# One fused attention and mixing kernel: the same instructions in another written order, with fixed PSUM places and buffers

## The chip, the cores and the metric

The kernel runs on one core of a Trainium2 chip. The metric is the device time of one execution in microseconds (us); lower is better. The core has five engines that each work through their own queue in order: TensorE (PE in the profile; its weight loads stand as PEld), VectorE (DVE), ScalarE (ACT), GpSimd (POOL) and SyncE (SP, which here issues the transfers). They wait for each other through semaphores.

## What is computed

Batch 4, 8 heads, sequence 768, head size 64. First a sparse attention, then a Fourier mixing and an MLP over 512 columns:

```
# attention, per batch b and head h; blocks of 64 keys, top_k = 3
k_rep = k.reshape(B, H, 12, 64, D).mean(axis=3)
gate  = einsum('bhsd,bhnd->bhsn', q, k_rep), blocks of the future at -1e9
mask  = (block of key in the 3 best of the query, or its own block) and key <= query
attn  = softmax(where(mask, q @ k.T / sqrt(D), -1e9));  x = attn @ v
# mixing, on x as (B, S, 512)
u   = x + real(fft(fft(x, axis=1), axis=2))
un  = (u - mean(u)) / sqrt(var(u) + 1e-6)
out = u + max(un @ w_ch1, 0) @ w_ch2          # 512 -> 2048 -> 512
```

## The kernel before

The work is cut into 16 pairs of heads (pair P belongs to batch P // 4) and 4 batches. One long string, `ORDER`, names every step; the program reads it once from left to right and emits the instructions of each step, so that the string sets the order in each of the five queues. A step is written `name:indices`. An engine takes its own steps in that order and nothing overtakes. The names are:

- Loads on SP: `Lk`, `Lq`, `Lv` bring k, q and v of a pair (`load`); `LF`, `LT`, `Lc`, `Li` bring constants. `W:c` and `X:c` bring pieces of the two MLP weights through GpSimd's queue (`load_w1`, `load_w2`); `W:0`, `W:1`, `W:2` hold the column tiles 0 to 3, 4 to 9 and 10 to 15 of the first weight.
- Preparing a pair: `tk`, `tq` transpose k and q on PE (pairs 0 to 6; from pair 7 on `kb` and `qc` turn blocks on VectorE instead). `ks` sums k over blocks, `kh` copies the sums (VectorE); `kc` copies k for the scores (ScalarE), `qc` copies q (VectorE) and `qs` copies it on (GpSimd).
- The gate: `g` on PE, then on VectorE `gt`, `gx` (the largest values), `gl:P,0` and `gl:P,1` (which blocks are out) and `gm`, which gives the mask tile mt. From pair 7 on, `K` on GpSimd spreads mt beside q.
- Scores and output: `s:P,i` makes one of six score tiles of a pair in PSUM; `e:P,i` takes the exponential on ScalarE (five wide ones of 1024 columns and a narrow one of 256, `e:P,5`); `d:P,i` clears the part above the diagonal (GpSimd); `vc` casts v (GpSimd); `v:P` multiplies with v on PE; `x:P` divides (VectorE) and writes x.
- Mixing of a batch: `fs`, `fd`, `f` fold x on VectorE; `y:b,h` and `m:b,k` are the two transforms on PE; `ty` (ScalarE) and `tr` (VectorE) copy what `y` made, `u:b,k` adds and sums (VectorE), `xu:b,k` scales (ScalarE). The result is transposed by `xt` on PE and `un` on VectorE for batch 0, by transfers (`un`) for the others. `bn`, `nv`, `nr` make the variance's root, `pg` is a small wait on GpSimd.
- MLP: `w:b,i` makes one of 16 hidden tiles (lines 641 and 643), `r:b,i` its relu (ScalarE, every fourth on VectorE); `c:b,t,h` is the second product, `o` adds and `od` stores.

PSUM holds four places of [128, 1024] fp32. Before, every PSUM tile takes the next of the four in the order of the string (`pst`: one tag, `bufs=4`), so a tile waits until the readers of the fourth tile back are done. SBUF buffers go round likewise: 3 for loads of k and of q, 2 for loads of v, 2 for q in fp32, 4 for mt, 2 for the exponentials (pt, one per pair), 5 for u.

```
    def pst(shape, name, dtype=FP):
        return psump.tile(shape, dtype, tag="ps", name=name)
...
    with tc.manual_schedule(engines={ET.SP, ET.PE, ET.DVE, ET.Activation, ET.Pool}):
        consts_first()
        for x in ORDER.split():
            n, a = x.split(":")
            WORK[n](*[int(i) for i in a.split(",")])
```

## Time and profile before

| | |
|---|---|
| median of 3 runs | 293.21 us (292.3 to 293.62) |
| span of the profiled execution | 290.3 us; the page gives no other time of it |
| granted TensorE clock | 1.00 throughout |
| busy: PE, DVE, ACT, POOL | 274.3, 203.0, 164.4, 113.2 us |
| instructions on PE, DVE, ACT, POOL | 2525, 606, 205, 286 |
| first matmul of the MLP | 65.35 us |

The page's slices divide the span into 40 parts of 7.26 us; a digit is the busy share in tenths. Matmuls are pipelined: a matmul of 512 columns stands with 379 ns, while eight of them in a row take 1.73 us, so PE's work is taken here from the starts of what follows, not from the durations. Rows of the timeline begin with start and duration in us, then engine, line, operation, output and inputs, and the count merged into the row; what stands in brackets is the idle time just ahead and what ended it. A row of a window gives the window, its length and the busy time and instructions of PE, PEld, DVE, ACT and POOL, then the granted clock, the share of the DMA engines and GB/s.

### The profile page before, as it was taken

How to read it: one execution, taken by the hardware profiler on the slowest of the kernel's cores; microseconds unless marked ns; L12 is line 12 of the kernel's file. 1: busy time of each engine (PE TensorE's matmuls, PEld its weight loads, DVE VectorE, ACT ScalarE, POOL GpSimd, SP SyncE). 2: the span in 40 equal slices, each digit the busy share in tenths (PEclk: the TensorE clock that was granted, in tenths of full speed). 3: DMA queues.
4: the chain of work that ended last, by engine and by line, in shares of the span. 5: the costliest groups of instructions: out<-in, count | busy, mean ns of one | idle time of the engine just before them, and what ended most of it. 6: DMA issues, size and time to landing. Idle time of an engine off the chain costs nothing.

```text
span 290.3 us, 6581 instructions
## 1 busy us (share of the span) xinstructions
PE 274.3 (94%) x2525; PEld 167.7 (58%) x2525; DVE 203.0 (70%) x606; ACT 164.4 (57%) x205; POOL 113.2 (39%) x286
## 2 busy tenths in 40 slices
PE   7696976899999999999999999999999999999995
PEld 3554664575656665565576457646766654656443
DVE  2899988999789988689988668609691559202122
ACT  3676878877579666579888505687143231263000
POOL 2246470614988815845760489414400001100000
PEclk9999999999999999999999999999999999999999
DMA  9999999899999399964900004541000024000034
GB/s 200 267 236 263 172 215 178 140 180 162 154 189 205 76 183 212 130 131 117 213 17 2 0 0 148 109 92 73 2 2 0 36 76 108 0 2 0 0 147 181
DMA packets 121423, 33.52 MB, mean 115 GB/s; under 512 B 114160, under 2 KB 118192, under 8 KB 121392
## 3 DMA queue, kind: packets, MB, share of 16 engines
q1 hardware_dynamic: 115728, 28.47, 46.0%
q0 software_dynamic: 3664, 4.19, 9.2%
q10 hardware_dynamic: 2000, 0.44, 0.7%
q8 instruction: 20, 0.33, 0.5%
q14 instruction: 11, 0.09, 0.1%
HBM read 28.63 MB, written 6.29 MB: 120 GB/s over the span
## 4 chain that ended last, share of the span: by engine, by line
PE 79%; DVE 13%; ACT 5%; issue 2%; DMA 1%; DVEq 0%; ACTq 0%
PE c L668 27%; PE h L641 19%; PE h L643 10%; PE sc L426 7%; PE av L461 4%; ACT pt L443 4%; DVE u L578 2%; PE yp L531 2%; DVE kr L306 2%; DVE q L328 2%; PE warmps L705 1%; PE sc L421 1%; DVE mx L378 1%; PE c L660 1%; PE g L354 1%
## 5 line engine op out<-in xcount | busy, mean ns | idle before, releaser
L443 ACT ACTIVATE pt<-sc 128x1024 f16<-128x1024 f32 (+1 forms) x96 | 83.5, 918 | 26.1 <-PE sc L426 14.6
L641 PE MATMUL h<-unT,w 128*128 128x512 f16 x256 | 84.5, 379 | 0.0
L668 PE MATMUL c<-w_sb,hT 128*128 128x512 f16 x368 | 83.0, 379 | 0.2 <-ACT pt L443 0.2
L643 PE MATMUL h<-unT,w 128*128 128x256 f16 x256 | 69.7, 272 | 0.0
L449 POOL TENSOR_SCALAR_AFFINE_SELECT pt<-pt 128x256 f16<-128x256 f16 x96 | 38.5, 424 | 68.0 <-ACT pt L443 45.9
L668 PEld LDWEIGHTS <-hT 128*128 128x128 f16 x368 | 35.7, 98 | 40.6 <-issue 0.7
L653 ACT ACTIVATE hT<-h 128x768 f16<-128x768 f32 x48 | 37.4, 809 | 34.7 <-PE h L643 34.6
L641 PEld LDWEIGHTS <-w 128*128 128x128 f16 x256 | 25.0, 98 | 29.5 <-issue 0.7
L680 DVE SCALAR_TENSOR_TENSOR u<-c,rs,u 128x512 f32<-128x512 f32 (+1 forms) x25 | 17.3, 724 | 29.9 <-PE c L668 25.6
L651 DVE TENSOR_SCALAR hT<-h 128x768 f16<-128x768 f32 x16 | 15.2, 948 | 19.4 <-PE h L643 19.4
L643 PEld LDWEIGHTS <-w 128*128 128x128 f16 x256 | 25.0, 98 | 3.9
L426 PE MATMUL sc<-qk 96*128 96x512 f16 (+3 forms) x144 | 26.0, 306 | 0.1
L224 POOL TENSOR_SCALAR_AFFINE_SELECT qk<-q 64x768 f16<-64x768 f32 (+1 forms) x25 | 21.0, 843 | 12.8 <-DVE q L328 12.1
L590 ACT ACTIVATE x<-u,nm 128x512 f16<-128x512 f32 x24 | 16.0, 714 | 16.3 <-DVE nm L584 16.2
L224 POOL TENSOR_SCALAR_AFFINE_SELECT qk<-mt 32x160 f16<-32x160 f16 x72 | 23.0, 340 | 2.6 <-DVE mt L398 0.9
L461 PEld LDWEIGHTS <-pt 128*128 128x128 f16 x672 | 22.2, 97 | 2.8 <-issue 1.1
L461 PE MATMUL av<-v,pt 128*128 128x65 f16 x672 | 23.0, 193 | 0.5 <-ACT pt L443 0.3
L421 PE MATMUL sc<-qk 64*128 64x512 f16 (+3 forms) x112 | 14.9, 306 | 5.4 <-ACT pt L443 3.2
L578 DVE SCALAR_TENSOR_TENSOR u<-mx,x 128x512 f32<-128x512 f32 x24 | 15.6, 685 | 5.2 <-PE mx L565 5.2
L224 POOL TENSOR_SCALAR_AFFINE_SELECT v<-nat 128x768 f16<-128x768 f32 x16 | 14.7, 920 | 8.6 <-DMA nat<-in_v_dram 8.6
L426 PEld LDWEIGHTS <-qk 96*128 96x128 f16 x144 | 12.7, 97 | 8.6 <-issue 0.9
L544 ACT CAST ty<-yp 128x772 f16<-128x772 f32 x8 | 8.0, 1036 | 16.7 <-PE yp L531 16.4
(98 smaller groups left out, 349.2 us busy)
## 6 DMA issues: line engine op xcount, KB each, us to landing
nat<-in_v_dram SPq DMA_DIRECT2D x16, 384.0 KB, 5.0
...
```

The costliest lines, as they stand in the source:

```text
L224: nc.gpsimd.affine_select(out=out, in_=in_, pattern=[[0, i] for i in n], base=0, channel_multiplier=0, compare_op=ALU.is_ge, fill=0.0)
L421: nc.tensor.matmul(ps[:, e, co:co + q1 - q0], qk[hs[e], 1, XW(P), 128 * jt:128 * jt + 128], qk[hs[e], 0, XW(P), q0:q1], start=(co == 0), s ...
L426: nc.tensor.matmul(ps[:, e, co:co + q1 - q0], qk[0:96, e, 1, 128 * jt:128 * jt + 128], qk[0:96, e, 0, q0:q1], start=True, stop=True)
L443: nc.scalar.activation(out=d["pt"][:, o:o + 2 * n].rearrange("p (e c) -> p e c", e=2), in_=d["sc", i][:, :, 0:n], func=AF.Exp, scale=0.125)
L449: nc.gpsimd.affine_select(out=dg, in_=dg, pattern=[[0, 2], [1, 128]], base=0, channel_multiplier=-1, compare_op=ALU.is_ge, fill=0.0)
L461: nc.tensor.matmul(av[:, e, 66 * st:66 * st + 65], pt[:, co:co + 128], vv[:, e, jt, 0:65], start=(cnt == 0), stop=(cnt == 20))
L578: nc.vector.scalar_tensor_tensor(out=u_b[:, k2, :].rearrange("p (m two) -> p two m", two=2), in0=mps[:, k2, :].rearrange("p (two m) -> p t ...
L641: nc.tensor.matmul(hp[:, 0:512], w1s, unT[:, dt, 0:512], start=(dt == 0), stop=(dt == NDT - 1))
L643: nc.tensor.matmul(hp[:, 512:768], w1s, unT[:, dt, 512:768], start=(dt == 0), stop=(dt == NDT - 1))
L653: nc.scalar.activation(out=hT, in_=hp, func=AF.Relu)
L668: nc.tensor.matmul(c_ps[b, g[0]][:, st - g[0], :], h_t[b, it][:, 128 * st:128 * (st + 1)], w2_sb[:, it, :], start=(it == 0), stop=(it == N ...
L680: nc.vector.scalar_tensor_tensor(out=o, in0=ps, scalar=st_t[b][1][:, st:st + 1], in1=o, op0=ALU.mult, op1=ALU.add)
```

## The change

The string holds the same 1002 steps before and after, each once. They stand in another order from the first load on, in all five queues. A step may now carry `@n`, and the new variable `place` holds that number while the step is emitted. It names the PSUM place (four tags with one buffer each, in place of one tag with four), the load buffer (0 to 2 for k and for q, 0 and 1 for v), the buffer of q in fp32 (0, 1), of mt (0 to 3), of the exponentials (0, 1) and of u (0 to 4). The numbers of buffers and their sizes are as before. The string is cut here after the part around the first tiles of the MLP.

```diff
@@ -110,70 +110,78 @@


 ORDER = """
-Lk:1 Lq:1 Lk:2 Lq:2 Lq:3 Lk:3 tk:0 ks:0 kh:0 iz:1 iz:0 tq:0 kc:0 qc:0 g:0 tq:1 gt:0 gx:0 gl:0,0
-gl:0,1 gm:0 qc:1 tk:1 kc:1 tk:2 kc:2 ks:1 qs:0 qs:1 Lq:4 Lv:0 Lk:4 Lv:1 kh:1 s:0,1 ks:2 s:0,3 tq:2
-qc:2 g:1 kh:2 e:0,1 s:0,0 s:0,5 gt:1 s:0,4 s:0,2 tk:3 e:0,3 e:0,5 g:2 gx:1 gl:1,0 Lq:5 Lk:5 gl:1,1
-gm:1 s:1,4 tq:3 s:1,3 e:0,0 tq:4 gt:2 tk:4 e:0,4 ks:3 qc:3 gx:2 gl:2,0 s:1,0 kh:3 qc:4 gl:2,1 s:1,1
-e:0,2 g:3 ks:4 e:1,4 gm:2 Lv:2 d:0,3 qs:2 d:0,4 d:0,2 vc:0 vc:1 d:0,0 d:0,1 d:0,5 Lv:3 Lq:6 LF:0
-Lq:7 Lk:6 Lk:7 LT:0 v:0 s:1,5 s:2,4 e:1,3 kc:3 tq:5 e:1,0 s:2,5 s:2,2 e:1,1 gt:3 kc:4 gx:3 gl:3,0
-kh:4 x:0 e:1,5 g:4 s:1,2 s:2,3 e:2,4 e:2,5 qc:5 gl:3,1 e:2,2 gt:4 e:1,2 tk:5 gx:4 gm:3 ks:5 e:2,3
-s:2,1 e:2,1 qs:4 qs:3 vc:2 d:1,4 d:2,5 qs:5 d:1,0 d:1,3 d:1,5 d:1,2 d:1,1 fs:0,0 kh:5 gl:4,0 fs:0,1
-gl:4,1 v:1 x:1 s:3,1 s:2,0 s:3,4 g:5 kc:5 s:3,3 e:3,1 e:3,4 s:3,0 qc:7 gm:4 e:2,0 tq:6 e:3,0 s:3,5
-e:3,5 e:3,3 gt:5 s:3,2 s:4,1 e:3,2 fs:1,1 gx:5 fs:1,0 gl:5,0 Lv:4 Lq:8 Lk:8 Lv:5 Lc:0 d:3,1 d:2,1
-d:2,2 d:3,4 d:2,0 d:3,5 d:3,0 d:2,3 d:2,4 vc:3 d:3,2 d:3,3 gl:5,1 kb:7 v:2 e:4,1 kc:7 gm:5 ks:7 v:3
-s:4,5 e:4,5 s:4,0 qc:6 x:2 s:5,4 e:5,4 s:5,5 s:4,4 x:3 s:5,2 s:4,3 s:5,0 tk:6 e:5,5 fs:2,0 kh:7
-fs:3,1 fs:3,0 fs:2,1 fd:3,0 fd:2,0 fd:2,1 fd:3,1 f:0,2 f:0,0 f:0,1 y:0,0 e:4,4 ks:6 f:0,3 y:0,1
-e:5,2 s:5,3 e:5,0 e:4,0 tr:0,0 e:4,3 tr:0,1 m:0,2 kc:6 ty:0,0 g:7 ty:0,1 kh:6 m:0,1 u:0,2 g:6 u:0,1
-s:4,2 gt:6 e:5,3 m:0,0 s:5,1 xu:0,2 e:4,2 xu:0,1 xt:0,1 gx:6 e:5,1 u:0,0 xu:0,0 Lk:9 Lq:9 W:0 W:1
-d:4,0 pg:0 vc:4 d:4,4 d:5,0 qs:6 d:4,3 d:4,1 W:2 d:4,2 d:4,5 gl:6,0 gl:6,1 v:4 un:0,1 gm:6 s:6,3
-gt:7 xt:0,0 xt:0,2 s:6,1 s:6,4 x:4 e:6,3 s:6,2 e:6,2 un:0,0 un:0,2 gx:7 gl:7,0 gl:7,1 kb:8 w:0,6
-r:0,6 w:0,12 e:6,1 w:0,11 w:0,2 qc:8 ks:8 gm:7 kb:9 kh:8 g:8 r:0,12 s:6,0 r:0,11 s:6,5 w:0,0 e:6,4
...
+Lk:1@1 Lk:2@2 tq:0@1 Lq:1@1 tk:0@2 iz:1 qc:0@0 tk:1@3 ks:0 Lq:2@2 qs:0 kh:0 ks:1 g:0@0 Lk:4@0
+tk:2@1 gt:0 kc:1 ks:2 kc:0 tq:1@0 Lq:4@0 gx:0 kc:2 gl:0,0 iz:0 qc:1@1 tq:2@3 Lk:3@1 gl:0,1 kh:1
+qs:1 gm:0@0 s:0,0@2 qc:2@0 s:0,4@1 Lk:7@2 e:0,0@0 g:1@0 qs:2 s:0,3@3 e:0,4 gt:1 s:0,1@2 d:0,0
+tk:4@0 e:0,3 kh:2 gx:1 d:0,4 g:2@1 gl:1,0 e:0,1 Lv:0@0 tk:3@3 gl:1,1 gt:2 kc:4 Lq:3@1 gm:1@1
+s:1,2@1 gx:2 kc:3 s:0,5@2 ks:4 e:0,5 e:1,2@1 s:0,2@2 d:0,5 ks:3 tq:4@0 Lv:1@1 e:0,2 s:1,4@1 gl:2,0
+Lk:5@0 vc:0 qc:4@1 s:1,3@3 e:1,4 s:1,0@2 d:0,3 kb:7 d:0,2 e:1,0 tq:3@0 d:1,2 gl:2,1 d:0,1 v:0@1
+kh:3 e:1,3 gm:2@2 Lq:5@2 qc:3@0 d:1,3 LF:0 s:1,5@2 s:2,3@3 kh:4 e:1,5 vc:1 x:0 Lv:3@0 g:3@0 e:2,3@0
+s:2,2@2 qs:3 gt:3 s:1,1@1 e:2,2 s:2,5@3 Lq:6@0 g:4@0 fs:0,1 gx:3 e:2,5 tq:5@2 e:1,1 d:2,5 gl:3,0
+d:1,0 s:2,1@3 gt:4 d:1,5 tk:5@1 e:2,1 d:1,1 qc:5@0 s:2,4@0 d:1,4 s:2,0@3 e:2,4 gl:3,1 Lv:2@1 fs:0,0
+v:1@2 gm:3@3 vc:3 ks:5 Lk:6@1 e:2,0 s:3,4@0 qs:5 gx:4 s:3,0@3 e:3,4@1 gl:4,0 d:2,1 x:1 d:2,2 e:3,0
+Lq:7@1 s:3,3@0 d:2,0 kh:5 ks:7 vc:2 g:5@2 kc:5 s:3,1@3 gl:4,1 e:3,3 d:2,3 gt:5 tq:6@1 d:2,4 LT:0
+d:3,4 s:3,5@2 gm:4@0 e:3,1 v:2@0 Lk:10@0 qs:4 qc:6@0 e:3,5 d:3,0 gx:5 s:3,2@3 d:3,3 s:4,2@2 d:3,1
+x:2 e:3,2 s:4,0@1 e:4,2@0 gl:5,0 s:4,1@3 d:3,2 qc:7@1 d:3,5 v:3@0 e:4,0 W:0 fs:2,0 Lv:5@0 gl:5,1
+fs:2,1 e:4,1 gm:5@1 s:4,4@2 fs:1,0 tk:6@1 Lv:4@1 x:3 e:4,4 s:5,0@3 fd:2,0 kc:6 s:5,2@0 fs:1,1
+s:4,3@2 fs:3,1 e:5,0@1 fs:3,0 fd:2,1 fd:3,0 s:4,5@3 e:4,5 fd:3,1 e:4,3 s:5,4@3 f:0,1 e:5,4 f:0,0
+s:5,5@2 e:5,5 y:0,0@3 f:0,2 Lk:9@1 ks:6 f:0,3 s:5,3@2 ty:0,0 y:0,1@1 kb:10 vc:4 e:5,2 Lq:9@2 tr:0,0
+d:4,2 kc:7 s:5,1@0 d:4,4 tr:0,1 d:5,2 m:0,2@3 W:1 kh:6 kh:7 ks:10 ty:0,1 Lk:8@2 d:4,3 d:4,1 u:0,2@0
+e:5,1 d:5,4 m:0,1@1 d:4,0 e:5,3 m:0,0@0 u:0,1@1 xu:0,2 g:6@3 d:5,3 d:5,0 xt:0,2@2 d:4,5 u:0,0@2
+xu:0,1 d:5,5 d:5,1 v:4@1 W:2 gt:6 xu:0,0 xt:0,1@0 qs:6 un:0,2 xt:0,0@3 un:0,1 qs:7 g:7@2 un:0,0
+Lc:0 x:4 w:0,6@0 vc:5 gx:6 Lq:8@0 w:0,5@3 r:0,6 kb:8 w:0,0@1 gl:6,0 r:0,5 gt:7 ks:8 w:0,2@0 gl:6,1
+kb:9 w:0,8@2 r:0,2 gm:6@2 gx:7 r:0,0 s:6,5@3 s:6,1@0 kh:10 kh:8 r:0,8 gl:7,0 v:5@1 e:6,1@0 gl:7,1
+qc:9@0 s:6,3@2 Lv:6@1 e:6,5 gm:7@3 K:7 s:6,2@0 e:6,3 x:5 w:0,11@3 Lv:7@0 e:6,2 bn:0,0 s:6,4@2
+s:6,0@1 qc:8@1 e:6,4 w:0,7@0 Lq:10@1 r:0,11 qs:8 kc:9 g:8@2 bn:0,1 w:0,12@3 e:6,0 gt:8 d:6,5 d:6,1
+Li:0 s:7,2@2 r:0,7 X:0 r:0,12 w:0,15@1 ks:9 e:7,2@1 d:6,0 qs:9 s:7,0@0 Lk:11@1 kh:9 r:0,15 s:7,5@3
+w:0,14@2 e:7,0 pg:0 gx:8 vc:7 e:7,5 s:7,3@1 r:0,14 gl:8,0 d:6,2 g:9@0 gl:8,1 s:7,4@3 d:6,3 fs:4,0
+X:1 w:0,3@2 qc:10@1 e:7,4 d:6,4 gt:9 e:7,3 d:7,2 s:7,1@3 d:7,5 gm:8@0 w:0,10@0 bn:0,3 e:7,1 d:7,3
+d:7,0 bn:0,2 d:7,4 kc:10 w:0,4@1 vc:6 gx:9 d:7,1 bn:0,4 v:6@3 r:0,10 K:8 Lk:12@0 r:0,3 r:0,4 v:7@0
+kc:8 gl:9,0 fs:5,0 x:6 w:0,9@1 gl:9,1 w:0,1@2 gm:9@1 K:9 r:0,9 x:7 s:8,5@3 g:10@1 fs:6,1 r:0,1
+w:0,13@0 bn:0,5 e:8,5@0 gt:10 s:8,2@2 r:0,13 kb:11 s:9,4@3 s:8,0@1 e:8,2 fs:7,0 c:0,0,0@0 fs:4,1
+gx:10 e:8,0 gl:10,0 nv:0 e:9,4@1 s:9,1@2 fs:7,1 Lv:9@0 nr:0 s:8,1@1 fs:6,0 fs:5,1 s:9,2@3 fd:6,1
+e:8,1 c:0,0,1 Lq:11@2 gl:10,1 fd:7,0 e:9,1 fd:6,0 fd:7,1 e:9,2 s:9,3@1 f:1,1 s:8,3@2 f:1,0 c:0,1,0
+e:8,3 Lv:8@1 f:1,3 e:9,3 Lq:13@0 f:1,2 s:9,0@3 d:9,4 s:9,5@2 ks:11 d:9,3 s:8,4@1 qs:10 c:0,1,1
+e:8,4 gm:10@2 kh:11 kb:12 e:9,5 e:9,0 d:8,3 y:1,1@1 Lk:13@2 d:8,0 o:0,1 kc:11 pg:1 c:0,2,0@2 d:9,0
+tr:1,1 vc:9 qc:11@0 Lq:12@1 ty:1,1 d:8,4 d:9,5 y:1,0@3 d:8,1 o:0,0 d:8,5 g:11@1 od:0,1 qs:11 ty:1,0
...
 assert PT_W == 5376 and len(COL) == 42

@@ -206,13 +214,15 @@
     dr = {n: nc.inline_tensor(C[n], name=f"c_{n}") for n in C}

     cpool = ctx.enter_context(tc.tile_pool(name="cst", bufs=1))
-    psump = ctx.enter_context(tc.tile_pool(name="psum", bufs=4, space=bass.MemoryType.PSUM))
+    psump = ctx.enter_context(tc.tile_pool(name="psum", bufs=1, space=bass.MemoryType.PSUM))
     apool = ctx.enter_context(tc.tile_pool(name="attn", bufs=2))
     bpool = ctx.enter_context(tc.tile_pool(name="bat", bufs=1))
     spool = ctx.enter_context(tc.tile_pool(name="small", bufs=3))

+    place = [0]
+
     def pst(shape, name, dtype=FP):
-        return psump.tile(shape, dtype, tag="ps", name=name)
+        return psump.tile(shape, dtype, tag=f"ps{place[0]}", name=name)

     def ctile(shape, dtype, name):
         return cpool.tile(shape, dtype, tag=f"c_{name}", name=name)
@@ -265,11 +275,11 @@
         b, hp = divmod(P, NP)
         src = (q, k, v)[who]
         if who == 2:
-            t = apool.tile([128, 2 * NST, 64], FP, tag="nat2", name=f"nat2_{P}", bufs=2)
+            t = apool.tile([128, 2 * NST, 64], FP, tag=f"nat2{place[0]}", name=f"nat2_{P}", bufs=1)
             eng.dma_start(t, src[b, 2 * hp:2 * hp + 2].rearrange("e (st p) d -> p (e st) d", p=128))
             nat[P, 2] = t
             return
-        t = apool.tile([128, NST, 2, 64], FP, tag=f"nat{who}", name=f"nat{who}_{P}", bufs=3)
+        t = apool.tile([128, NST, 2, 64], FP, tag=f"nat{who}{place[0]}", name=f"nat{who}_{P}", bufs=1)
         nat[P, who] = t
         if P in BLK[who]:
             nat[P, who] = t = t.rearrange("p st e d -> p (st e d)")
@@ -320,7 +330,7 @@
                 nc.scalar.copy(out=qk[0:64, e, 1, :], in_=ps[64 * e:64 * e + 64])

     def a_q32(P):
-        q32 = apool.tile([128, S], FP, tag="q32", name=f"q32_{P}")
+        q32 = apool.tile([128, S], FP, tag=f"q32{place[0]}", name=f"q32_{P}", bufs=1)
         pairs[P]["q32"] = q32
         if P in BLK[0]:
             nc.vector.transpose(out=q32, in_=nat[P, 0])
@@ -394,7 +404,7 @@

     def g_back(P):
         d = pairs[P]
-        d["mt"] = apool.tile([128, 288 if P < NX else 160], F16, tag="mt", name=f"mt_{P}", bufs=4)
+        d["mt"] = apool.tile([128, 288 if P < NX else 160], F16, tag=f"mt{place[0]}", name=f"mt_{P}", bufs=1)
         nc.vector.transpose(out=d["mt"], in_=d["lt"])

     def stage_K(P):
@@ -438,7 +448,7 @@
     def s_exp(P, i):
         d = pairs[P]
         if "pt" not in d:
-            d["pt"] = apool.tile([128, PT_W], F16, tag="pt", name=f"pt_{P}")
+            d["pt"] = apool.tile([128, PT_W], F16, tag=f"pt{place[0]}", name=f"pt_{P}", bufs=1)
         o, n = SC_OFF[i], sum(q1 - q0 for (_, q0, q1) in SC_TILES[i])
         nc.scalar.activation(out=d["pt"][:, o:o + 2 * n].rearrange("p (e c) -> p e c", e=2),
                              in_=d["sc", i][:, :, 0:n], func=AF.Exp, scale=0.125)
@@ -567,7 +577,7 @@

     def m_u(b, kp):
         mps, x_b = m_ps[b, kp], x_t[b]
-        u_t[b, kp] = u_b = bpool.tile([128, 2, DM], FP, tag="u_b", name=f"u{kp}_{b}", bufs=5)
+        u_t[b, kp] = u_b = bpool.tile([128, 2, DM], FP, tag=f"u_b{place[0]}", name=f"u{kp}_{b}", bufs=1)
         if b not in st_t:
             un_t[b] = bpool.tile([128, NDT, S], F16, tag="unT", name=f"unT_{b}", bufs=1)
             st_t[b] = [bpool.tile([128, *sh], FP, tag=n, name=f"{n}_{b}", bufs=2)
@@ -688,7 +698,7 @@
     def consts_first():
         for who in (1, 0):
             src = (q, k)[who]
-            t = apool.tile([128, NST, 2, 64], FP, tag=f"nat{who}", name=f"nat{who}_0", bufs=3)
+            t = apool.tile([128, NST, 2, 64], FP, tag=f"nat{who}{place[0]}", name=f"nat{who}_0", bufs=1)
             nat[0, who] = t
             for e, eng in ((0, nc.sync), (1, nc.scalar)):
                 eng.dma_start(t[:, :, e, :], src[0, e].rearrange("(st p) d -> p st d", p=128))
@@ -765,6 +775,8 @@
     with tc.manual_schedule(engines={ET.SP, ET.PE, ET.DVE, ET.Activation, ET.Pool}):
         consts_first()
         for x in ORDER.split():
+            x, _, at = x.partition("@")
+            place[0] = int(at or 0)
             n, a = x.split(":")
             WORK[n](*[int(i) for i in a.split(",")])

```

## The prediction

> **What bounds the kernel now.** I read the page's busy lines and slices first, then TensorE's work in two windows, then the chain and the timelines of the stage before the second window.

> ```profile
> PE 274.3 (94%) x2525; PEld 167.7 (58%) x2525; DVE 203.0 (70%) x606; ACT 164.4 (57%) x205; POOL 113.2 (39%) x286
> PE   7696976899999999999999999999999999999995
> DVE  2899988999789988689988668609691559202122
> ...
> 0.00:65.35 65.35, 52.83 (x769) 36.00 (x770) 56.01 (x192) 47.12 (x58) 26.21 (x64) 1.00 1.03 205
> 65.35:287.00 221.65, 221.34 (x1758) 131.66 (x1756) 146.52 (x415) 117.25 (x147) 87.02 (x222) 1.00 0.43 89
> ...
> 62.35 0.39 PE L421 MATMUL sc<-qk 64*128 64x384 f16 x4
> 62.88 1.07 PE L597 MATMUL xt<-id,x 128*128 128x128 f16 x16
> 64.02 0.39 PE L421 MATMUL sc<-qk 64*128 64x256 f16 x4
> 65.35 0.39 PE L641 MATMUL h<-unT,w 128*128 128x512 f16 x1
> ```

> From 65.35 us on, when the first matmul of the MLP (`w:0,6`) starts, PE is busy for 221.3 of 221.7 us at full clock. A changed order can save nothing there; it can only add waits. Before that PE is busy for 52.8 of 65.35 us while VectorE is at eight or nine tenths in most slices. So the change is worth what it does to one moment: how early `w:0,6` can start, less the PE work that it leaves until afterwards.

> That work is counted in the two orders. Ahead of `w:0,6` both have the 14 transposed loads, `g:0` to `g:7`, all score tiles of pairs 0 to 5, `v:0` to `v:4` and the whole Fourier part of batch 0. The old order also has four score tiles of pair 6 (`s:6,3`, `s:6,1`, `s:6,4`, `s:6,2`), the new one none. By the last four rows these take 62.88 - 62.35 = 0.53 and 65.35 - 64.02 = 1.33, together 1.86 us, which move behind the start.

> **When `w:0,6` starts in the new order.** No instruction is added or removed, so all durations come from this trace. I carry the new order along the engines' queues, each item starting when its queue is free, its inputs are there and its PSUM place has been read out.

> ```profile
> 5.06 1.79 PE L297 MATMUL tp<-id,nat 128*128 128x128 f32 x12
> 8.77 0.69 PE L347 MATMUL g<-q,kr 128*32 128x288 f32 x8 [1.92 <-DVE q L328]
> 12.50 2.08 ACT L443 ACTIVATE pt<-sc 128x1024 f16<-128x1024 f32 x2
> ...
> 6.57 0.89 DVE L306 TENSOR_REDUCE kr<-tp 128x12 f32<-128x768 f32 x1
> 7.67 0.95 DVE L328 COPY q<-tp 128x768 f32<-128x768 f32 x1
> 9.52 0.48 DVE L361 STREAM_TRANSPOSE gt<-g 128x288 f32<-128x288 f32 x1 [0.90 <-PE g L347]
> 10.24 0.72 DVE L378 MAX8 mx<-gt 128x8 f32<-128x8 f32 x9
> 11.56 0.48 DVE L398 STREAM_TRANSPOSE mt<-lt 128x288 f16<-128x288 f16 x1
> ```

> *To the first exponential: later.* `tq:0` now goes ahead of `tk:0`, and its load lands near 6.0 (in the old order `tq:0` follows `tk:0` in the 12 transposes from 5.06). VectorE then does `qc:0`, `ks:0`, `ks:1` (0.9 each) from 7.05 to 9.8, with `g:0` on PE from 9.05; `gt:0` 0.75, `ks:2` 0.9, `gx:0` 0.7, `gl:0,0` 0.3, `qc:1` 0.9, `gl:0,1` and `kh:1` 0.3, `gm:0` 0.45: mt is there at 14.2, and `e:0,0` starts at 14.7 against 12.50. `ks:1`, `ks:2` and `qc:1` are done by then, which the old order still had ahead of it.

> ```profile
> 12.50:40.30 27.80, 23.43 (x364) 15.49 (x363) 26.74 (x96) 22.52 (x27) 15.00 (x30) 1.00 1.05 229
> ...
> 38.46 2.21 ACT L443 ACTIVATE pt<-sc 128x256 f16<-128x256 f32 x3 [0.36 <-PE sc L433]
> 42.29 1.02 ACT L443 ACTIVATE pt<-sc 128x1024 f16<-128x1024 f32 x1 [1.61 <-PE av L461]
> ...
> 46.26 5.88 ACT L443 ACTIVATE pt<-sc 128x1024 f16<-128x1024 f32 x7 [1.11 <-PE sc L433]
> ...
> 40.73 2.73 PE L461 MATMUL av<-v,pt 128*128 128x65 f16 x84 [0.33 <-ACT pt L443]
> ...
> 43.76 0.96 DVE L221 TENSOR_TENSOR x<-av,rcp 128x768 f16<-128x768 f32 x1
> ```

> *Pairs 0 to 3: caught up.* ScalarE is the measure here. From `e:0,0` to `e:3,2` it has 20 wide exponentials, 4 narrow ones and 3 copies of k; at 0.91 (the six wide and one narrow of the 5.88 us row, the narrow one at about 0.3), 0.3 and 0.75 that is 21.6 us. In the old order this stretch ends at 38.46 + 2.21 = 40.67, after 28.2 us; the window shows ScalarE busy for 22.5 of its first 27.8 us. In the new order I find waits of 0.35 before `e:1,4`, 0.3 before `e:1,5`, `e:2,3` and `e:3,4`, 0.45 before `e:2,1`, 0.35 before `e:2,4` and 0.95 before `e:3,2` (its score tile stands behind `v:2`): 3.0 us. So it ends at 14.7 + 21.6 + 3.0 = 39.3. It waits less because pair 4 is transposed ahead of pair 3 and score tiles of the next pair stand between those of the last one.

> Behind it the old order runs `v:2` and `v:3` together (2.73 us from 40.73), so `x:2` and `x:3` queue on VectorE and the last ends at 43.76 + 0.96 = 44.7; `e:4,1` waits 1.61 us for `v:2`, which still reads its buffer. The new order has `v:2` at 36.6 and `x:2` done at 39.3. GpSimd's `d:3,2` and `d:3,5` let `v:3` go at 40.3; it ends at 41.6, `x:3` at 43.15, and `e:4,2` runs straight after `e:3,2`. By the end of this part 1.55 us are won.

> ```profile
> 44.99 0.89 DVE L221 TENSOR_TENSOR sd<-x 128x384 f16<-128x384 f16 x3
> 45.80 1.96 DVE L221 TENSOR_TENSOR zw<-sd 128x768 f16<-128x768 f16 x4
> 47.79 0.56 DVE L221 TENSOR_TENSOR fg<-zw 128x762 f16<-128x762 f16 x1
> 52.08 2.04 DVE L550 CAST tr<-yp 128x768 f16<-128x768 f32 x2
> 55.36 0.68 DVE L578 SCALAR_TENSOR_TENSOR u<-mx,x 128x512 f32<-128x512 f32 x1
> 63.88 1.28 DVE L602 COPY unT<-xt 128x1024 f16<-128x1024 f16 x2
> ...
> 43.21 1.67 ACT L320 CAST qk<-nat 64x768 f16<-64x768 f32 x2
> 53.15 2.05 ACT L544 CAST ty<-yp 128x772 f16<-128x772 f32 x2 [0.31 <-DVE tr L550]
> 56.90 1.33 ACT L590 ACTIVATE x<-u,nm 128x512 f16<-128x512 f32 x2 [0.82 <-DVE nm L584]
> ...
> 51.72 1.35 PE L531 MATMUL yp<-fs_sb,fg 128*128 128x193 f16 x14
> ```

> *From `x:3` to `w:0,6`: shorter.* The old order takes 65.35 - 44.7 = 20.65 us. In the new one VectorE folds from 43.15 (four `fd` at 0.47, three `fs` at 0.27, two `f` at 0.56) to 47.0. ScalarE runs `e:4,2` to `e:4,4` until 43.1, `kc:6` and `e:5,0` until 44.75, waits 0.55, then `e:4,5`, `e:4,3`, `e:5,4` until 47.4, which frees the place of `y:0,0`: 47.6 to 49.1. `s:5,3`, then `y:0,1` until 50.6. ScalarE: `ty:0,0` to 50.2, `e:5,2` to 51.1, `kc:7` 1.6 to 52.7, `ty:0,1` to 53.6. That copy sets the end: `m:0,1` from 53.8 to 54.65, `m:0,0` to 55.55 (0.87 each); `m:0,2` and `u:0,2` were done by 54.4. `u:0,1` to 56.3 and `u:0,0` to 57.7 (1.4 each: two of 0.68 and the mean); `xu:0,0`, behind the other two at 1.25, to 59.15; `xt:0,0` to 59.85; `un:0,0`, the last of three at 0.6, to 60.65. `w:0,6` starts 0.2 later (63.88 + 1.28 to 65.35 in the old one): 60.8, 17.65 us after `x:3`. The old order is held up by `m:0,0`, which stands on PE behind `g:6` and `s:4,2`, and by four score tiles of pair 6 and `x:4` on VectorE ahead of the last two `un`.

> *The sum.* 65.35 - 60.8 = 4.55 us earlier, 1.86 us of scores behind it: 2.7 us won. After it I followed 45 us of handovers, to `y:1,0`. Inputs arrive 0.1 to 4 us ahead, but at eight places PE takes a PSUM place within 0.1 us of its last reader's end (`w:0,15` after `e:6,0`, `s:7,1` after `e:7,4`, `s:9,2` after `e:9,4` and the like). No row shows such tight handovers at that place; nothing is gained by them, and the bound above is below. I charge 0.4 us, nearest to the second window's total of 0.3 us of idle. Net 2.3 us: span 290.3 - 2.3 = 288.0. The median of the runs, 293.21, lies 2.9 us above the span (the page has no other time for the profiled execution); I keep that distance: 290.9 us, 0.8% less.

> Loads change places too: `Lk:7` and `Lk:10` come early, `Lq:3` and `Lv:0` behind `Lk:7`. On SP they keep ahead of their first use by 2 us or more as I count them, and their cover is the exponentials; `Lk:8` waits for `kc:7`, with `Lc` and `Lq:8` queued behind, first needed 9 us later. The one load that could end last is a rival.

> **The rivals.**

> ```profile
> PE sc L421 <- ACT pt L443: 3.2, 5, 1.6
> POOL v L224 <- DMA nat<-in_v_dram: 8.6, 3, 6.3
> ...
> 41.91 1.71 POOL L735 DMA_DIRECT2D w<-in_moe_w_ch_dram  x2
> 55.35 0.76 POOL L735 DMA_DIRECT2D w<-in_moe_w_ch_dram  x1
> DMA to landing us min/median/max: 7.9/8.0/10.9
> ```

> *Tight places.* Each of the eight handovers after `w:0,6` waits for ScalarE. In the first stage such waits are 3.2 us in 5, 0.64 each. At 0.3 each they cost 2.4 us instead of 0.4 and the time is 292.9, no change; at 0.64 they cost 5.1 and it is 295.6. Against it: ScalarE is busy for 117 of the 222 us of the second window, and the old order, also fed by four places, shows no such loss there. Chance 0.22, most of it on no change.

> *The weights last: slower.* `W:1` brings the columns of `w:0,6`. In the old order it is the second issue from 41.91, 22 us ahead of need. In the new one it stands on GpSimd behind `vc:4` and `d:5,2` and goes out at about 51.5; with 7.9 to 10.9 us to landing it is there at 59.4 to 62.4, against a need at 60.8. The worst of this costs 62.4 + 0.2 - 60.8 = 1.8 us. But if `vc:4` waits for its load of v as long as the longest wait of its kind (6.3 us), `W:1` goes out at 57.8, lands at 65.7 to 68.7, and PE stands idle: 290.9 + 5.1 to 8.1 = 296.0 to 299.0. It decides from a landing after 60.6, and eats the whole gain from one after 62.9. Against it: `Lv:4` is issued near 36, seven us before I have `vc:4` reach it. Chance 0.12.

> [...] The rows above show 7.9 us at the least, so I keep its chance.

> **How the numbers follow.** Forecast 0.66; tight places 0.22; weights 0.12. Low end: no charge for handovers and half of ScalarE's 3.0 us of waits gone as well, 2.7 + 1.5 = 4.2: 289.0. High end: it takes in no change and the start of both rivals' slower parts, 293.9. About 0.5% is what a measurement can tell here, 291.7 to 294.7. Faster holds the forecast less its upper edge, 0.64; within, 0.23 (tight places at 0.3, part of a late `W:1`); slower, 0.13.

> **What would show it.** The first exponential near 14.7; `v:2` near 36.6, ahead of the last exponential of pair 3; `x:3` ending near 43; the first h near 60.8 with no score of pair 6 ahead of it; PE at 9.9 or more of 10 us from 61 on; `W:1` landed before the last `un`. I am wrong if h starts after 63, if PE is idle for over 2 us behind it, or if VectorE, not ScalarE, holds back `y:0,0`.

## The result, and the profile after

The change makes the kernel slower: 296.6 us (median of four executions, 295.38 to 297.88) against 292.79 us for the kernel before beside it, a ratio of 1.0124 with a 95% interval of 1.0087 to 1.0161. 290.9 us had been forecast, with a range from 289.0 to 293.9. Ratios here and below leave out, on both sides, executions that took over 1.5% more than the fastest of the same kernel. The profiled execution took 295.38 us, with a span of 293.7 us; in that of before the span was 290.3 us.

These lines of the page of the changed kernel answer to those of before; the windows are in the second fence (the last two count PE alone), PE's timeline in the third.

```profile
PE 275.3 (94%) x2525; PEld 168.5 (57%) x2525; DVE 197.0 (67%) x606; ACT 164.4 (56%) x205; POOL 113.5 (39%) x286
PE   6699897869999999997999999999999999999995
DVE  2989998997998886998678756923562560750131
...
PEclk9999997999999999999999999999999999999999
```

```profile
64.06:290.30 226.24, 223.98 (x1792) 132.55 (x1791) 141.86 (x434) 118.71 (x148) 83.08 (x214) 1.00 0.43 89
...
44.91:48.33 3.42, 1.44 (x22) 1.00 1.26 243
48.33:51.74 3.41, 3.41 (x30) 0.50 1.03 183
```

Three things are new. The clock row has a 7: from 48.33 to 51.74 us TensorE was granted half its clock, where the trace of before shows 1.00 throughout. PE's row has a 6 at 59 to 66 us, where the row of before has 9, and a 7 at 132 to 140 us. And from the first h tile to its last step PE is idle for 226.24 - 223.98 = 2.26 us instead of 0.31.

```profile
45.41 0.23 PE L431 MATMUL sc<-qk 64*128 64x128 f16 x2 [0.70 <-ACT pt L453]
...
46.19 0.39 PE L431 MATMUL sc<-qk 64*128 64x512 f16 x2 [0.50 <-ACT pt L453]
...
47.10 0.23 PE L431 MATMUL sc<-qk 64*128 64x128 f16 x2 [0.33 <-ACT pt L453]
...
48.02 1.05 PE L541 MATMUL yp<-fs_sb,fg 128*128 128x193 f16 x7 [0.64 <-ACT pt L453]
...
50.31 0.53 PE L541 MATMUL yp<-fs_sb,fg 128*128 128x193 f16 x2
50.78 0.61 PE L431 MATMUL sc<-qk 64*128 64x384 f16 x4
...
62.14 0.40 PE L607 MATMUL xt<-id,x 128*128 128x128 f16 x4 [1.54 <-ACT x L600]
...
64.06 0.38 PE L651 MATMUL h<-unT,w 128*128 128x512 f16 x1 [0.51 <-DVE unT L612]
...
71.49 0.22 PE L443 MATMUL sc<-mt,indz 64*128 64x32 f16 x4 [0.61 <-DVE mt L408]
```

`y:0,0` starts at 48.02 and the tile behind it at 50.78: 2.76 us for what takes 1.62 at full clock (in e1 below). `w:0,6` starts at 64.06, 1.29 us earlier than before and not 4.55.

```profile
58.15 0.17 DVE L594 TENSOR_SCALAR nm<-sm 128x2 f32<-128x2 f32 x1
...
59.56 1.76 DVE L594 TENSOR_SCALAR nm<-sm 128x2 f32<-128x2 f32 x1
61.24 0.47 DVE L371 STREAM_TRANSPOSE gt<-g 128x288 f32<-128x288 f32 x1
...
67.48 0.98 DVE L311 STREAM_TRANSPOSE nat<-nat 128x768 f32<-128x768 f32 x1 [1.71 <-DMA nat<-in_k_dram]
```

```profile
58.91 0.76 POOL L745 DMA_DIRECT2D w<-in_moe_w_ch_dram  x1
59.68 2.50 POOL L234 TENSOR_SCALAR_AFFINE_SELECT qk<-q 128x768 f16<-128x768 f32 x3
```

```profile
119.74 2.56 SPq L287 DMA_DIRECT2D nat<-in_q_dram  x4
122.41 2.60 SPq L615 DMA_TRANSPOSE unT<-x  x2
125.11 0.54 SPq L279 DMA_DIRECT2D nat<-in_v_dram  x1
125.75 5.29 SPq L615 DMA_TRANSPOSE unT<-x  x4
```

```profile
PE h L653 <- DMA unT<-x: 1.6, 1, 1.6
```

These are the timelines of VectorE, GpSimd and SP's queue, and a line of the waits (in total, times, longest). On VectorE the two elements of nm, 0.17 us after `u:0,1`, take 1.76 us after `u:0,0`, while GpSimd issues `W:2` and runs `qs:6` and `qs:7`. Both `xu:0,0` and the 1.54 us of idle PE at 62.14 wait for them. Later VectorE waits 1.71 us for the load `Lk:8` with the mask of pair 6 queued behind it, and SP's queue sends `Lq:15` ahead of the transposes `un:1`, for which PE then waits 1.59 us.

The account: the last step, `c:3,5,0`, starts at 288.34 us instead of 285.21, 3.12 us later. That is 1.29 us won ahead of h, 1.86 us of score tiles moved behind it, and a remainder of 2.55 us of new waits behind it (the 1.59, the 0.61, and small ones). The expectations below count otherwise: against an estimate of the work alone, from start to start (220.25 us in the new order, 218.38 in the old), PE is idle for 4.03 us between `w:0,6` and the last step (4.35 to the very end), against 1.48 in before.

### The profile page after: what moved, and what is told of

The parts are those of the page before. It is cut to its first block, busy times and chain, and to the rows that moved or that the text cites. A ratio compares the mean times of both kernels' runs of the same rounds, so it can differ in the third digit from the quotient of the medians.

```text
span 293.7 us, 6588 instructions
## 1 busy us (share of the span) xinstructions
PE 275.3 (94%) x2525; PEld 168.5 (57%) x2525; DVE 197.0 (67%) x606; ACT 164.4 (56%) x205; POOL 113.5 (39%) x286
## 4 chain that ended last, share of the span: by engine, by line
PE 79%; DMA 7%; ACT 6%; DVE 3%; SPq 2%; issue 1%; ACTq 0%; DVEq 0%
PE c L678 27%; PE h L651 17%; PE h L653 9%; PE sc L436 7%; PE av L471 6%; ACT pt L453 5%; DMA nat<-in_k_dram 4%; DMA nat<-in_q_dram 2%; PE yp L541 2%; PE sc L431 2%; SPq L287 2%; PE tp L307 2%; PE sc L443 1%; DMA unT<-x 1%; PE mx L575 1%; PE mx L574 1%
## 5 line engine op out<-in xcount | busy, mean ns | idle before, releaser
L653 PE MATMUL h<-unT,w 128*128 128x256 f16 x256 | 69.8, 273 | 1.6 <-DMA unT<-x 1.6
L663 ACT ACTIVATE hT<-h 128x768 f16<-128x768 f32 x48 | 37.6, 812 | 47.4 <-PE h L653 47.1
L459 POOL TENSOR_SCALAR_AFFINE_SELECT pt<-pt 128x256 f16<-128x256 f16 x96 | 37.1, 410 | 26.1 <-ACT pt L453 22.5
L234 POOL TENSOR_SCALAR_AFFINE_SELECT qk<-q 64x768 f16<-64x768 f32 (+1 forms) x25 | 20.5, 823 | 12.4 <-DVE q L338 10.9
L471 PE MATMUL av<-v,pt 128*128 128x65 f16 x672 | 22.5, 193 | 0.0
L231 POOL TENSOR_TENSOR t<-vr,rs 128x6 f32<-128x6 f32 x12 | 3.2, 270 | 47.5 <-DVE rs L631 46.9
```

Source lines behind the costliest of these rows:

```text
L234: nc.gpsimd.affine_select(out=out, in_=in_, pattern=[[0, i] for i in n], base=0, channel_multiplier=0, compare_op=ALU.is_ge, fill=0.0)
L459: nc.gpsimd.affine_select(out=dg, in_=dg, pattern=[[0, 2], [1, 128]], base=0, channel_multiplier=-1, compare_op=ALU.is_ge, fill=0.0)
L471: nc.tensor.matmul(av[:, e, 66 * st:66 * st + 65], pt[:, co:co + 128], vv[:, e, jt, 0:65], start=(cnt == 0), stop=(cnt == 20))
L653: nc.tensor.matmul(hp[:, 512:768], w1s, unT[:, dt, 512:768], start=(dt == 0), stop=(dt == NDT - 1))
L663: nc.scalar.activation(out=hT, in_=hp, func=AF.Relu)
```

## The experiments

The four causes were first mended one at a time. In the diffs a stretch of the string is broken into lines so that the moved steps stand alone.

**e1: the clock.** A step `sa` makes a score tile once more in its old tile.

```diff
 s:4,3@2
+sa:5,2@0
 fs:3,1 e:5,0@1 fs:3,0 fd:2,1 fd:3,0 s:4,5@3
+sa:5,2@0
 e:4,5 fd:3,1 e:4,3 s:5,4@3
+sa:5,2@0
 f:0,1 e:5,4 f:0,0 s:5,5@2
+sa:5,2@0
 e:5,5 y:0,0@3
```

> The changed kernel, with the score tile s:5,2 computed again, into the same place and with the same values, behind s:4,3, s:4,5, s:5,4 and s:5,5: about 0.57 us of TensorE work in each of the four gaps (0.70, 0.50, 0.33 and 0.64 us) between 44.7 and 48.0 us; nothing waits for the repeats but TensorE itself. Theory (the idle stretch halves the clock): the granted clock stays 1.0 from 43 to 53 us, y:0,0 takes 1.5 us instead of 2.8 and ends at 49.5-49.7, ty:0,0 starts 1.2 earlier, w:0,6 starts at 62.7-63.2 instead of 64.06, and the span falls by 0.9-1.3 us, to 292.4-292.8. Rival (the clock dip comes from something else than idleness, such as the load of the stretch before): the dip to half stays at 48.3-51.7, y:0,0 still takes 2.6-2.8, and the span is the same or up to 0.5 us more.

```profile
44.10:47.51 3.41, 3.03 (x58) 1.00 1.22 221
```

```profile
48.02 0.76 PE L541 MATMUL yp<-fs_sb,fg 128*128 128x193 f16 x7 [0.23 <-ACT pt L453]
...
49.38 0.33 PE L541 MATMUL yp<-fs_sb,fg 128*128 128x193 f16 x2
...
68.67 0.38 PE L651 MATMUL h<-unT,w 128*128 128x512 f16 x1 [1.20 <-DVE gt L376]
```

First a window, then PE's timeline. The theory holds: work that computes nothing new makes the changed kernel faster. The clock is 1.00 throughout, `y:0,0` ends at 49.71 instead of 50.84, `w:0,6` starts at 62.11, the span is 292.3 us, and the ratio to before 1.0062 (1.0034 to 1.009). Of the 1.95 us won ahead of h, 0.33 is a shorter nm operation (1.43 us). Only 1.4 of the 1.95 us reach the end. The last row shows why: `w:0,8` takes place 2, which `gt:7` has to read first, and `gt:7` stands on VectorE behind the wait for `Lk:8`.

**e2: GpSimd.** The copies go to where GpSimd waits for a load.

```diff
 y:0,1@1 kb:10
+qs:6 qs:7 vc:5
 vc:4
...
-qs:6
...
-qs:7
...
-vc:5
```

> The changed kernel with the GpSimd copies qs:6, qs:7 and vc:5 put ahead of vc:4 on GpSimd, into its wait from 41.3 to 50.3 us, so that no GpSimd copy runs at 59.7-63.2. Theory (VectorE's 0.17 us operation on nm is held up by the GpSimd copies beside it): the nm operation of u:0,0 takes 0.15-0.4 us instead of 1.76, xu:0,0 starts at 59.8-60.1 instead of 61.36, w:0,6 at 62.4-62.8 instead of 64.06, span down by 1.2-1.6 us. Price of the move: small operations of fs and fd at 42-46 us can be stretched in their place, up to 0.5 us each, which could take back up to 1 us through y:0,0. Rival (the nm operation waited for something of its own, the sums of u:0,0 for instance): it still ends at 61.3, and h starts at 64.0.

```profile
48.56 2.54 POOL L234 TENSOR_SCALAR_AFFINE_SELECT v<-nat 128x768 f16<-128x768 f32 x2 [1.02 <-DMA nat<-in_v_dram]
...
45.20 2.75 DVE L231 TENSOR_TENSOR zw<-sd 128x768 f16<-128x768 f16 x3
...
49.00 0.88 DVE L516 COPY fg<-zw 128x6 f16<-128x6 f16 x1
```

The nm operation takes 0.17 us again, and `xu:0,0` follows at once. But the price was above the bound that I gave: three `fd` take 2.75 us instead of 1.49 and a copy of six columns 0.88 instead of 0.18, each while a GpSimd copy runs. `f:0,0` ends 1.9 us later, `w:0,6` starts at 64.74, and the ratio is 1.0203 (1.0134 to 1.0272). Part of this is the clock: in the profile it is halved for two windows, 48.12 to 54.95 us, and `y:0,0` takes 3.03 us. The hold-up was moved, not removed.

**e3: SP's queue.**

```diff
 xu:1,0
-Lq:15@1
 kh:12 gx:11
...
 un:1,2
+Lq:15@1
 c:0,2,1
```

> The changed kernel with the load Lq:15 (four DMAs, 2.56 us of SP's queue) moved behind un:1,2, so that the transposes un:1,0 to un:1,2 of batch 1 leave SP's queue 2.5 us earlier. Theory (SP's queue holds the first task that reads unT of batch 1): un:1,2 is issued by 128.6 instead of 131.1 us, TensorE's wait of 1.59 us at w:1,8 goes, and the span falls by 1.4-1.8 us, to 291.9-292.3. Rival (the transposes are bound by their own time or the wait is covered by other work behind it): another wait takes its place and the span stays within 0.4 us of 293.7.

PE no longer waits for unT: it is busy for 10.00 us between 130 and 140 instead of 8.41, and from `w:1,8` to the last step it takes 154.52 us instead of 156.46. The profiled execution is longer all the same, 296.0 us: h starts only at 68.12, behind three stretches at half clock (14, 38 and 52 us) and an nm operation of 2.13 us. The ratio is 1.0057 (1.0029 to 1.0085). The four longest of its ten executions took 297.7 us or more, at a mean clock of 0.982 to 0.988; with them the ratio of the medians is 1.0097.

**e4: the load ahead of the mask.**

```diff
 r:0,6
-kb:8
 w:0,0@1 gl:6,0 r:0,5 gt:7
-ks:8
 w:0,2@0 gl:6,1 kb:9 w:0,8@2 r:0,2 gm:6@2
+kb:8 ks:8
```

> The changed kernel with kb:8 and ks:8 moved behind gm:6 on VectorE, so that VectorE no longer waits 1.71 us for the load Lk:8 ahead of the mask of pair 6. Theory: gm:6 ends at 68.5-69.8 us instead of 71.44, the 0.73 us before s:6,5 go, and the idle time of TensorE behind w:0,6 falls from 4.35 to 3.2-3.6; span down by 0.6-1.0 us. Rival (the wait is made good by the tasks of the feed-forward, which have no hurry): nothing in the span moves by more than 0.3 us, because the mask of pair 7 or 8 is late in its place.

```profile
130.47:133.88 3.41, 1.41 (x12) 1.00 0.56 98
133.88:137.29 3.41, 3.41 (x13) 0.50 0.83 168
```

```profile
PE h L653 <- DMA unT<-x: 2.0, 1, 2.0
```

Two windows of PE, and the waits behind them. `gm:6` ends at 67.78 and `s:6,5` waits for nothing; at `w:0,11` the order is 1.09 us ahead (0.31 of it already at `w:0,6`). At `w:1,8` PE then waits 2.0 us for SP's queue, and this wait is followed by 3.41 us at half clock, in a stretch where PE has no slack: idle time between `w:0,6` and the last step is 5.5 us by the estimate of the work, where 3.2 to 3.6 was expected. Ratio 1.0035 (1.0005 to 1.0066).

**When the clock halved.** This is counted from the clock records and the PE rows of the 14 traces here. In all 14 profiles the granted clock changes only at multiples of 3.413 us after it first became full (in before it is full for 286.72 us, 84 of them, to past the span's end; in the changed kernel for 44.37 us, 13 of them, then half for one and full for 71), and the phase of these windows differs from execution to execution (the clock first became full 4.99 us into the span of before, 3.95 us into that of the changed kernel). Over the 1130 windows up to 286 us, PE's busy time (from the starts and durations of its rows) was at most 1.76 us in the 13 that were followed by half clock, and at least 1.77 us in every other (1.77 us in before's first, from 4.99 us). The 1.41 us at 130.47 above is one of the 13, and the changed kernel's 1.44 us at 44.91 another. The window of before at the same place is just above the bound:

```profile
42.50:45.91 3.41, 1.86 (x50) 1.00 0.95 137
```

No long gap was in it: the largest idle stretch in the window at 44.91 was 0.70 us. In the trace of before a window would hold 1.76 us or less if it started within 0.88 us (43.35 to 44.23; and for some 2 us near 6 us); in that of after within 1.16 us (44.08 to 45.24) and again within 1.97 us (59.24 to 61.21, the wait for nm). The mean clock of an execution, with all executions counted, fits: 0.998 or more in 43 of 81 executions of the kernel before, and in none of 8 of the changed kernel, in 8 of 9 of e1. In the kernel before, the median span is 290.3 us in these 43 executions and 291.35 in the other 38.

**The changed kernel again.**

> The changed kernel itself, unaltered, as the measure for the three beside it on the same chip. Expected 294-298 us, 1.008 to 1.016 of the kernel before; its granted clock 0.988 to 1.0, and where a run has 1.0 a span of 291-292.5.

```profile
61.61:65.03 3.42, 1.49 (x18) 1.00 1.25 210
65.03:68.44 3.41, 3.41 (x13) 0.50 1.23 219
```

Ratio 1.0119 (1.0025 to 1.0212). Here the phase spared the stage of `y:0,0`; the window that held the wait for nm, with 1.49 us of work, was followed by half clock just as h began, and `w:0,6` to `w:0,0` took 4.28 us instead of 2.60.

**e5 and e6: three together, and other places.** e5 is e1, e3 and e4 in one. e6 has three of the repeats and exchanges places 1 and 3 from `y:0,0` on (`y:0,0@1`, `y:0,1@3` and so forth).

> Three of the four edits together: s:5,2 repeated in the four gaps, kb:8 and ks:8 behind gm:6, Lq:15 behind un:1,2. Theory (the lost time is the half clock at 48 us, the late load Lk:8 ahead of the mask of pair 6, and SP's queue ahead of the transposes, and each covers for the other when it is mended alone): w:0,6 at 62.1 us, idle time of TensorE behind it 1.5-2.5 us instead of 4.03, last task at 284.0-285.2, span 289.0-290.5, at or below that of the kernel before. Rival (other loads are as late behind these): idle time behind w:0,6 stays over 3.5 us and the span at 291.0-292.5.

> The repeats of s:5,2 (three of them), and the PSUM places 1 and 3 exchanged for every tile from y:0,0 on, so that y:0,0 no longer waits for the exponential of s:5,4 to free place 3. Theory (the place costs what the wait of 0.64-0.83 us says): y:0,0 starts at 47.2-47.4 us, with f:0,0, instead of 48.02; w:0,6 at 61.3-61.7 instead of the 62.1 with the repeats alone; the span falls by less than that, 0-0.5 us below 292.3, since Lk:8 and SP's queue hold what follows. Rival (the place is no bound, the samples f are): y:0,0 starts at 47.9-48.1.

e5: 1.0039 (0.9998 to 1.0081). Its profiled execution missed my numbers: PE stood idle 2.15 us from 28.5 us on, ahead of `tq:5`, the clock was halved at 32 and again at 66 us, and `w:0,6` started at 66.91. Without a half clock (3 of 10 executions) the spans are 290.4 to 292.6 us.

e6 was a mistake of mine, and its trace says so:

```profile
47.92 0.95 DVE L316 TENSOR_REDUCE kr<-tp 128x12 f32<-128x768 f32 x1
...
48.93 0.76 PE L541 MATMUL yp<-fs_sb,fg 128*128 128x193 f16 x7 [1.41 <-DVE kr L316]
```

Place 1 is not free: `ks:6` on VectorE still reads the transposed k in it until 48.87, so `y:0,0` starts later than with place 3. Ratio 1.0108 (1.0054 to 1.0161).

**e7, e8, e9: the whole.** e7 joins e6, e5 and a first other order on GpSimd. e8 keeps the places as changed and orders GpSimd by what VectorE does beside it; e9 is e8 without the repeats, that is, the instructions of the changed kernel alone. The diff shows GpSimd's steps by themselves (the same in e8 and e9), and `ks:10`; `kb:8` and `Lq:15` move as in e4 and e3.

```diff
-vc:4 d:4,2 d:4,4 d:5,2 W:1 d:4,3 d:4,1 d:5,4 d:4,0
-d:5,3 d:5,0 d:4,5 d:5,5 d:5,1 W:2 qs:6 qs:7 vc:5
+vc:4 W:1 qs:6 d:4,2 d:4,4 d:4,3 qs:7 d:4,1 d:4,0
+d:4,5 d:5,2 d:5,4 W:2 d:5,0 d:5,5 d:5,1 d:5,3 vc:5
...
-ks:10
 ty:0,1
...
+ks:10
 kh:10
```

> All of it: repeats and exchanged places as in e6, kb:8 and Lq:15 moved as in e5, and on GpSimd vc:5 ahead of vc:4 (in the wait behind f:0,3, which goes ahead of ks:6), qs:6 behind d:4,5 and qs:7 behind W:1, so that at the nm operation of u:0,0 (57-58 us) GpSimd has only masks of 0.36 us. Theory: that operation takes 0.2-0.6 us instead of 1.4-1.8, w:0,6 starts at 60.0-61.0, idle time behind it 1.5-2.5, last task at 282.5-284.0, span 287.5-289.3: what the prediction gave for the change. Rival (GpSimd's copies only move the delay, as in e2, where they held up fs, fd and f): w:0,6 at 61.5-62.5 and a span of 289.5-291.

> The four repeats of s:5,2; kb:8, ks:8 behind gm:6; Lq:15 behind un:1,2; ks:10 out of the stage of batch 0 (to kh:10); and GpSimd's long copies where VectorE has only operations that the traces show undisturbed: W:1 and qs:6 behind vc:4, qs:7 behind three masks, W:2 ahead of the last four masks, vc:5 last. Theory: f:0,0 ends at 47.2 as in the changed kernel, the nm operation of u:0,0 takes 0.2-0.5 us, w:0,6 starts at 60.7-61.5 (62.1 in e1), idle time of TensorE behind it is 1.5-2.8 us; the span is 288.0-290.0 in runs at a clock of 1.0, 0.2-0.9% less than the kernel before at 1.0 (290.1). By the windows of 3.413 us on TensorE's clock seen in the profiles so far (one in which TensorE is busy for under 1.77 us is followed by one at half clock), few runs should show a dip: none is due to the stretches at 44 and at 59 us. Rival (the load of GpSimd moved ahead delays the masks, v:4 and u:0,2, and with them h): w:0,6 at 62 or later, and a span of 290 or more.

> The same without the repeats: the same instructions as the changed kernel, in another order. Theory of the windows: those of them that start between 44.1 and 45.2 us hold under 1.77 us of TensorE's work; as the windows start at a phase that differs from run to run, about a third of the runs (1.16 of 3.41) get a half clock at 48 us, with 1.2-1.9 us more span; the others equal e8 within 0.4 us. The median is 0-0.5 us above that of e8, the spread larger. Rival (the dip follows the phase of nothing, every run has it): all runs are 1.5 us above e8 and show a clock of 0.994 or less.

e7 went the rival's way, further than it said: `vc:5` met `fd` again (`f:0,0` ended 4.5 us after `x:3` instead of 3.8), the places cost what they cost in e6, and `w:0,6` started at 66.45; 1.0074 (1.004 to 1.0107). e8 and e9 give back the whole loss: 1.0007 (0.9973 to 1.0042) and 0.9998 (0.9958 to 1.0038).

```profile
58.73 0.22 DVE L594 TENSOR_SCALAR nm<-sm 128x2 f32<-128x2 f32 x1
...
59.37 1.47 DVE L231 TENSOR_TENSOR gt<-gt,lim 128x16 f32<-128x16 f32 x1
```

```profile
62.68:287.50 224.82, 223.91 (x1792) 132.71 (x1791) 143.77 (x434) 118.67 (x148) 83.54 (x214) 1.00 0.44 91
```

In e9 nm takes 0.22 us and h starts at 62.68 (`vc:5` still holds up `gt:6`, the second row, 1.47 us instead of 0.18, with the copies `un` behind it); PE is idle for 0.91 us behind it instead of 2.26; the span is 290.9 us. In e8 10 of 11 executions have no half clock. In e9 8 of 11 have one or more, where I had expected a third: why is open. The medians differ by no more than the noise all the same, so here the repeats gain nothing. e8's profile missed its numbers (h at 61.98 us with nm at 0.64 us beside the issue of `W:2`, span 293.0 us), and it has the fourth cause in another place:

```profile
114.73 0.98 DVE L336 STREAM_TRANSPOSE q<-nat 128x768 f32<-128x768 f32 x1 [1.76 <-DMA nat<-in_q_dram]
...
116.47 0.34 DVE L376 STREAM_TRANSPOSE gt<-g 128x160 f32<-128x160 f32 x1
116.86 0.27 PE L574 MATMUL mx<-fd_sb,ty 128*128 128x256 f16 x1 [1.17 <-DVE gt L376]
```

`qc:12` waits for its load, `gt:11` is queued behind it, place 1 stays taken, and `m:1,1` waits.

**e10 and e11.** e10 is e8 with three more moves; e11 is GpSimd's new order and the move of `ks:10` alone.

```diff
-Lv:5@0 gl:5,1 fs:2,1 e:4,1 gm:5@1 s:4,4@2 fs:1,0 tk:6@1 Lv:4@1
+Lv:4@0 gl:5,1 fs:2,1 e:4,1 gm:5@1 s:4,4@2 fs:1,0 tk:6@1 Lv:5@1
...
 W:1
+vc:5
...
-vc:5
...
+gt:11
 qc:12@1
...
-gt:11
```

> e8 with three more moves: Lv:4 loaded ahead of Lv:5 (places exchanged), vc:5 directly behind W:1 on GpSimd so that it does not run beside gt:6 (1.47 us instead of 0.18 for one operation in e9), and gt:11 ahead of qc:12 on VectorE, so that a late load Lq:12 no longer holds place 1 and with it m:1,1 (1.17 us in e8's profile). Theory: vc:4 starts by 49.0-49.5, w:0,6 at 60.7-61.6, idle time behind it 1.5-2.5 us, span 288.0-290.0 at a clock of 1.0, ratio to the kernel before 0.991-0.998. Rival (loads and copies that are moved collide elsewhere): w:0,6 at 62 or later and a ratio of 0.999-1.004, the same as e8.

> The changed kernel with GpSimd's order of e8 alone (W:1 and qs:6 behind vc:4, qs:7 behind three masks, W:2 ahead of the last four, vc:5 last) and ks:10 at kh:10; kb:8, Lq:15 as in the changed kernel, no repeats. It does again what e2 tried, without GpSimd's copies beside fs, fd and f. Theory (GpSimd holds up the nm operation of u:0,0, and through it h and the clock's window at 59-62 us): f:0,0 ends at 47.2-47.9, the nm operation takes 0.2-0.6 us, w:0,6 starts at 62.0-62.8 in a run without a dip, no window that would halve the clock starts between 58 and 62 us, and the median lies 1-2 us below that of the changed kernel: 294.5-296 where before has 292.8-293.2. Rival (what is won ahead of h is lost behind it, since Lk:8 and SP's queue keep their times): w:0,6 as early, but 296-297.

```profile
60.95 0.38 PE L651 MATMUL h<-unT,w 128*128 128x512 f16 x1 [0.37 <-DVE unT L612]
```

```profile
60.95:286.70 225.75, 223.90 (x1792) 132.75 (x1791) 143.89 (x435) 118.76 (x148) 83.22 (x214) 1.00 0.44 91
```

e10 starts h at 60.95 us, yet the span is 290.0 us and the ratio 1.0017 (0.9982 to 1.0051): the rival's number, the same as before. Behind h PE is idle for 1.85 us by the window, 3.4 by the estimate of the work (284.64 - 60.95 - 220.25), where I had 1.5 to 2.5; 0.7 of it for `un:1` and 0.7 for `x:5` stand in the list of waits, the rest in pieces under 0.3. e11 is at 1.0187 (1.0135 to 1.0239), no better than the changed kernel. In its profile the half clock at 49 us came first, everything behind it met other neighbours on GpSimd (nm 0.99 us, beside `vc:5`), and PE waited 2.1 us for `un:1`. So GpSimd's order is worth nothing by itself. Beside the other edits it may pay: e8 differs from e5 by this order and `ks:10` alone, with 1.0007 against 1.0039, but the intervals overlap.

## Why the prediction was wrong

**Right.** The first exponential started at 14.49 us (14.7 forecast), `v:2` at 37.03 (36.6), `v:3` at 40.65 (40.3); `e:3,2` ended at 40.08 (39.3), `x:3` at 43.37 (43.15). The wait for place 3 put `y:0,0` at 48.02 instead of 47.6, with the end of `e:5,4` at 47.97. The 1.86 us of scores behind h agree with the two estimates of the work (220.25 - 218.38 = 1.87). That ScalarE, not VectorE, holds `y:0,0` back is right. `W:1` landed at 60.6 and bound nothing, though `vc:4` waited 8.5 us for its load, longer than the 6.3 that I took as the worst (`Lv:4` went out at 42.5 us, not near 36). That rival stayed away by luck: it had 3.4 us to spare because h was late itself, and would have had 0.2 with h at 60.8. The 2.9 us between span and median is no fixed distance: in every execution that has both on record it is 1.7 to 1.9, so the profiled execution of before was about 1.1 us faster than that median; the forecast of 2.3 us less does not hang on it.

**The step that failed first: the chain from `x:3` to `w:0,6`.** It was summed with durations of the old trace, as if an operation cost the same beside any other. Two of its terms did not. `y:0,0` took 2.76 us at half clock (1.5 in the sum, 1.62 at full clock in e1), so `ty:0,0` started at 50.88 instead of 49.2 (0.4 us of it for the place) and the copies behind it as much later: 1.3 us, and e1 gave it back. The mean behind `u:0,0`, part of "1.4 each", took 1.76 us instead of 0.17: 1.6 us, and e9 gave it back. The start of VectorE's `u:0,2`, behind `ks:10`, adds 0.3. With the 0.4 for the place these make 3.6 us, where the start was 3.26 late; other terms came out a little shorter. e10, with the clock, nm and `ks:10` mended, started h at 60.95 us where the sum had 60.8. The steps of the chain were right but for `ks:10`; their durations were taken as if nothing that runs before or beside an operation could change them.

Of the clock, the grid of 3.413 us and the changing phase stand in every profile here. A look for long idle gaps would not have warned of the half clock: no gap in the window ahead of 48.33 was over 0.70 us, and about half a window's work was the bound (1.44 us in that window, at most 1.76 in all). Of VectorE beside GpSimd, the six-column copy of e2 (0.88 us instead of 0.18) ended 0.04 us after the GpSimd copy beside it, and that copy itself took 1.29 us instead of 0.90. nm waited longer, through the end of the issue of `W:2` (59.67) and two copies: it ended at 61.33 us, 0.03 after the second.

**The second: "only the start of `w:0,6` matters".** PE was saturated in the old order because that order had its loads and transposes in time for it. I charged 0.4 us for tight places; the change cost 2.55. The forecast named `Lk:8` with a cover of 9 us and did not carry it through; the last of its four transfers landed at 67.4, and VectorE reached it at 65.8. SP's order around `un:1` was beyond the 45 us that I followed. The rival of tight places named the right size with the wrong mechanism: what came late were loads and SP's queue, and a place passed that on to PE only where VectorE's reader stood behind such a wait (`gt:7`, `gt:11`).

**How much is shown.** That the moves of e9 (GpSimd's order with `ks:10`, SP's queue, `kb:8`) together give back the loss is shown. One by one, e4 shows that the place of `kb:8` costs time, and e1 that the half clock does, though its interval just touches that of the changed kernel (1.009 and 1.0087). For SP's queue the trace of e3 shows the wait gone, and the times do not settle it: with all ten executions the ratio of 1.0097 is within the changed kernel's interval. For GpSimd's order the traces show what it does to nm, and no run settles what it is worth in the total. How the 3.8 us divide is not shown either: the shares depend on the phase of the clock's windows, and e1, e3 and e4 have overlapping intervals. The clock is the weakest part of the sum: e9 gives back the loss with half clocks in 8 of 11 executions. Its six executions with a mean clock of 0.993 or 0.994 have spans from 290.0 to 293.9 us, its three at 1.0 from 290.2 to 291.6. Open is also why e9 meets so many half clocks, and where e10 loses what its early start should have brought: by the account that gives before's 285.2 us, its last step should start at 60.95 + 220.25 + 1.5 = 282.7 us, and it started at 284.6.
